# An S4 convolution and token mixer on one core: where the first half's transform back, its reads and the weights' splits stand

## The chip, the core and the metric

The kernel runs on one NeuronCore of a Trainium2 chip. The core has five engines that each work through their own list of instructions: TensorE (PE; its weight loads are shown as PEld), VectorE (DVE), ScalarE (ACT), GpSimd (POOL) and SyncE (SP). They wait for one another by semaphores. ScalarE, SP and POOL also issue DMAs, each on a queue of its own. The metric is the device time of one execution in microseconds.

## The reference

Everything is float32. B = 1, L = S = 2048, D = 512, N = 128, F = 1376.

```python
def _A_ref(u, A_re, A_im, B_re, B_im, C_re, C_im, log_dt, Dskip):   # S4 as a convolution
    dt = jnp.exp(log_dt)[:, None]
    A, Bc, Cc = A_re + 1j * A_im, B_re + 1j * B_im, C_re + 1j * C_im
    P = jnp.exp((dt * A)[:, :, None] * l[None, None, :])
    K = jnp.einsum("dn,dnl,dn->dl", Cc, P, dt * Bc).real
    # K and u are padded to 2L, their spectra multiplied, the product transformed back, cut to L
    return y + u * Dskip
def _B_ref(x, w1, w2, w3, w4):
    h = _gelu(_layernorm(x) @ w1)
    # four quarters of the channels are shifted by +1, -1, +2, -2 in time
    x1 = x + shifted @ w2
    return x1 + _gelu(_layernorm(x1) @ w3) @ w4
mod = (_silu(c) @ w_mod).reshape(c.shape[0], 6, 1, -1)             # sa, ca, ga, sb, cb, gb
x = A_u
x = x + ga * _A_ref(_layernorm(x) * (1 + ca) + sa, ...)
return x + gb * _B_ref(_layernorm(x) * (1 + cb) + sb, w1, w2, w3, w4)
```

## The kernel before, in words

The order of nearly all instructions is written out by hand (`tc.manual_schedule()`): an engine executes what its list says in the order of the program text, and only waits are put in by the framework.

**Stage 1** (to about 209 us) builds the convolution's kernel K in KX and the first transform of u, which goes to DRAM (VU). A table `side` (L506 and below) puts other work into its 32 rounds; among it are copies of w2, w3 and w4 from their input tensors to DRAM scratch (WD), issued by POOL.

**Stage 2** (209 to about 313 us) is the convolution in the frequency domain. `k_first` (L619), called eight times, transforms K into VK0 and VK1, with evictions by ScalarE and VectorE. Then sixteen steps follow, (jh, kc) for the two halves of the channels jh and eight blocks kc of frequencies. In step n the text has:

- `spectrum_k` (L664): TensorE's second transform of K, into psb banks. It uses T2 and its negative T3, which POOL writes (`flip`, L658).
- `multiply` (L685): six VectorE instructions, four products (ma, mb) and two sums (zc).
- `back` (L695) of step n-1: TensorE's transform of zc with Gm into psa banks (pz), ScalarE's eviction into z, and POOL's two DMAs of z to DRAM (ZT). There are two z buffers, so an eviction waits until the store of two steps earlier has landed.
- `spectrum_u` (L642) of step n+1: TensorE's transform of a VU block, which SP had loaded (`load_vu`, L638) into one of seven buffers ld, and ScalarE's three evictions (us).

The x that the result is added to (four DMAs, `load_x`, L723), FI, w1, w2 and the reads of ZT (`load_inv`, L717) are also issued by SP between the steps. `inverse` (L739) is the last transform back: `inv_half` (L726) multiplies blocks of ZT with FI on TensorE, and VectorE adds the result to x in X2 (which lies in KX). For the first half jh = 0 there are four parts g, each reading four of the eight ZT blocks: parts 0 and 3 read k = 0, 3, 4, 7 and parts 1 and 2 read k = 1, 2, 5, 6. Parts 0 and 3 stand in steps 12 and 13, part 1 in step 15, part 2 behind the steps.

Weights are split for TensorE into a high half (ScalarE writes it, w1h) and a low half (VectorE subtracts, w1l): `weights`, L743, with `load` and `split`. w1 is loaded in steps 8 and 9 into ld blocks and split in steps 9 and 10. w2 is loaded in step 12 and split in steps 14 and 15.

**The hole.** Behind step 15 its z must be stored and read back before anything of the second half jh = 1 can be transformed. In the meantime there are the transform back of (0, 2), statistics, and `keep` (L1162), matmuls whose results nobody reads.

**Stage 3** mixes tokens in eight groups of two blocks (`mix_mod1`, `mix_mod2`, `mix_norm`, `transposed`, `parts_of`, `mix_half`): the modulation and statistics on VectorE, the norm (h), the gelu (go) and the high half of the transposed norm (nh) on ScalarE, and the product with w1 on TensorE. go goes through DRAM (GD) and comes back shifted (win, `chan_load`); `chan_split` splits it (wh on ScalarE, the low half on VectorE), `chan_sum` multiplies it with w2. **Stage 4** (from about 375 us) is the channel MLP with w3 and w4.

Of the kernel before, what the change touches and what calls it, by code (L numbers as in the profile page):

```python
# [106 lines left out]
def body(ctx, tc, A):  # L107
# [12 lines left out]
    WD = {k: dpool.tile(list(A[k].shape), F32, name="D" + k) for k in ("w2", "w3", "w4")}  # L120
# [390 lines left out]
    for k in range(2):  # L511
        side[28 + 3 * k].append(lambda i=k * 256: P.dma_start(WD["w2"][i:i + 256], A["w2"][i:i + 256]))
# [94 lines left out]
    Gm = c2.tile([128, 2, 64], F32, name="Gm")  # L607
# [3 lines left out]
    ldp = a2.enter_context(pool("ldp", bufs=7))  # L611
# [44 lines left out]
    t3s = {}  # L656

    def flip(kc):  # L658
        t = t3s[kc] = c2.tile([128, 8, 64], F32, name="T3", bufs=3)
        for gh in range(2):  # L660
            r = slice(gh * 64, gh * 64 + 64)
            P.tensor_scalar(t[r], T2[kc // 4][r, kc % 4 * 4:kc % 4 * 4 + 8, 64 - gh * 64:128 - gh * 64], -1.0, None, op0=OP.mult)

    def spectrum_k(jh, kc):  # L664
        p = [kbank([128, 2, 2, 128]) for gh in range(2)]
        for i in range(2):
            for ro in range(2):
                for ri in range(2):
                    for kk in range(2):
                        for gh in range(2):  # L670
# [5 lines left out]
                            elif ro == ri:  # L676
                                w = w[:, gh * 64:gh * 64 + 64]
                            else:
                                w = t3s[kc // 2 * 2][rows, k1 % 8]
# [15 lines left out]
    def back(jh, kc):  # L695
        zc = zcs.pop((jh, kc))
        z = s2.tile([128, 4, 256], F32, name="z")
# [19 lines left out]
    def load_inv(jh, k, i=None, q=Y):  # L717
        if (jh, k) not in zis:
            zis[jh, k] = block()
# [3 lines left out]
    def load_x(g):  # L723
        Y.dma_start(X2[:, g * 4:g * 4 + 4].rearrange("p b d -> p (b d)"), A["x"][g])
# [18 lines left out]
    def weights(pl, src, rows, cols, name, ntile):  # L743
# [3 lines left out]
        def load(stage, i, m=1, c0=0, c1=cols):  # L747
            n = min(128, rows - i * 128)
            w = stage(m, c1 - c0) if stage else lo.bitcast(F32)[:, i:i + m, c0:c1]
            Y.dma_start(w[:n], src[i * 128:i * 128 + (m - 1) * 128 + n, c0:c1].rearrange("(a p) n -> p a n", p=n))  # L750

            def split():
                for j in range(m):
                    h = hi[:n, i + j, c0:c1]
                    act(h, w[:n, j])
                    V.tensor_sub(lo[:n, i + j, c0:c1], w[:n, j], h.bitcast(F32))  # L756
            return split
        return hi, lo, load

    def two(m, n):  # L760
        return block().rearrange("p (a c) b -> p a (c b)", a=2)
# [330 lines left out]
    def split_w(n):  # L1092
        for _ in range(n):
            splits.pop(0)()

    steps = [(jh, kc) for jh in range(2) for kc in range(8)]
    with tc.manual_schedule():
        load_vu(*steps[0])
        flip(0)
        Y.dma_start(Gm, A["G"].rearrange("p (a b) -> p a b", a=2))  # L1100
        for r in range(8):
            k_first(r)
            if r == 3:
                load_vu(*steps[1])
            if r == 6:
                load_vu(*steps[2])
        us = spectrum_u(*steps[0])
        split = None
        for n, st in enumerate(steps):
            p = spectrum_k(*st)  # L1110
            multiply(*st, us, p)
            if n == 7:
                v0x.close()
                pw2 = ctx.enter_context(pool("pw2", side="right", reuse_waits="tile"))
                pw1 = ctx.enter_context(pool("pw1", side="right", reuse_waits="tile"))
                W2h, W2l, ldw2 = weights(pw2, WD["w2"], 512, 512, "w2", 4)
# [185 lines left out]
```

## Time and profile before

| | us |
|---|---|
| median of 3 runs (lowest, highest) | 690.18 (689.29, 690.67) |
| profiled execution | 691.26 |
| its span | 689.5 |
| TensorE busy | 642.6 (93%) |
| VectorE busy | 498.0 (72%) |
| ScalarE busy | 331.2 (48%) |
| POOL busy | 124.8 (18%) |
| DMA: bytes moved, mean rate over the span | 86.42 MB, 125 GB/s |
| granted TensorE clock, mean of the span | 0.989 |

The engines' busy times overlap, and a busy TensorE is not TensorE at its peak, since matmuls are pipelined and their ends are modelled. The shares are means over four stages with different limits; what an edit is worth is read from its own stage. Times in the rows are microseconds from the start of the span. The last brackets of a row give the idle time of the engine ahead of the instruction and what ended it.

### The profile page before, as it was taken

To read this page: it belongs to the slowest core of one execution; us is meant where nothing else is said; L and a number is where in the kernel's file an instruction comes from. 1 tells how busy PE (TensorE), PEld (TensorE's weight loads), DVE (VectorE), ACT (ScalarE), POOL (GpSimd) and SP (SyncE) were. 2 spreads that over 40 slices of the span, in tenths; PEclk is the share of its full clock that TensorE was granted. 3 is DMA by queue.
4 is the path that set the end of the run, shared out by engine and by line. 5 is a ranking of instruction groups with operands and counts; after the bars stand their busy time and mean duration, and the time that the engine had idled before them with its cause. 6 is when DMAs were issued, how large, how long until landed. Compare 5 with 4: busy or idle time off the path is not lost.

```text
span 689.5 us, 16884 instructions
## 1 busy us (share of the span) xinstructions
PE 642.6 (93%) x7195; PEld 509.2 (74%) x7195; DVE 498.0 (72%) x795; ACT 331.2 (48%) x505; POOL 124.8 (18%) x236
## 2 busy tenths in 40 slices
PE   1899999999999998977998999999999999999996
PEld 0456655655569776634887889999899889898895
DVE  7899999999996887986987967464574536363522
ACT  3878988889875557432444623123131312222121
POOL 4011112112103355413741101001010000000000
PEclk9999999999999999998999999999999999999999
DMA  8603264643739997967387010020100201010001
GB/s 299 284 2 79 75 218 105 209 121 85 275 85 317 354 335 258 346 204 226 108 257 240 1 32 32 16 77 15 47 31 17 77 1 62 1 49 13 1 31 31
DMA packets 51091, 86.42 MB, mean 125 GB/s; under 512 B 4676, under 2 KB 39496, under 8 KB 48424
## 3 DMA queue, kind: packets, MB, share of 16 engines
q1 hardware_dynamic: 46712, 66.74, 30.1%
q0 software_dynamic: 3440, 17.57, 7.4%
q8 instruction: 56, 0.92, 0.6%
q10 hardware_dynamic: 864, 1.05, 0.5%
q14 instruction: 19, 0.16, 0.1%
HBM read 59.12 MB, written 32.90 MB: 133 GB/s over the span
## 4 chain that ended last, share of the span: by engine, by line
PE 70%; DVE 6%; DMA 5%; ACT 3%; POOL 2%; issue 1%; ACTq 0%; SPq 0%; DVEq 0%; POOLq 0%
PE pm L841 7%; PE pm L838 7%; PE pm L839 7%; PE xx L448 7%; PE pa L954 6%; PE pa L955 6%; PE pa L962 6%; PE kp L498 3%; DMA ZT<-z 3%; PE ph L893 2%; PE ph L895 2%; PE ph L892 2%; DMA ld<-ZT 2%; PE pu L426 2%; PE pT L803 2%; PE pk L626 2%
## 5 line engine op out<-in xcount | busy, mean ns | idle before, releaser
L115 ACT ACTIVATE gh<-pm 128x512 fp32r<-128x512 f32 (+1 forms) x48 | 26.9, 560 | 200.7 <-PE pm L841 200.7
L838 PE MATMUL pm<-nh,w3h 128*128 128x256 f32 (+1 forms) x352 | 86.6, 281 | 2.7 <-ACT nh L115 2.7
L839 PE MATMUL pm<-nh,w3l 128*128 128x256 f32 (+1 forms) x352 | 86.3, 280 | 0.1
L946 DVE TENSOR_TENSOR gl<-gf,gh 128x512 fp32r<-128x512 f32 (+1 forms) x48 | 30.8, 643 | 68.4 <-ACT gf L115 68.4
L954 PE MATMUL pa<-w4h,gh 128*128 128x512 f32 (+1 forms) x176 | 69.6, 395 | 0.0
L838 PEld LDWEIGHTS pm<-nh,w3h 128*128 128x128 f32 (+1 forms) x352 | 66.0, 187 | 4.4 <-ACT nh L115 2.9
L955 PE MATMUL pa<-w4l,gh 128*128 128x512 f32 (+1 forms) x176 | 68.9, 392 | 0.0
L839 PEld LDWEIGHTS pm<-nh,w3l 128*128 128x128 f32 (+1 forms) x352 | 65.9, 187 | 2.2 <-DVE w3l L756 0.5
L765 POOL TENSOR_TENSOR rs<-mv,eps_t 128x1 f32<-128x1 f32 (+1 forms) x39 | 11.0, 282 | 282.4 <-DVE mv L771 265.4
L841 PE MATMUL pm<-nl,w3h 128*128 128x256 f32 (+1 forms) x352 | 55.0, 278 | 0.0
L449 PE MATMUL xx<-MG,ON 64*128 64x512 f32 x160 | 48.1, 397 | 0.0
L962 PE MATMUL pa<-w4h,gl 128*128 128x512 f32 (+1 forms) x176 | 48.0, 390 | 0.0
L448 PE MATMUL xx<-MG,ON 64*128 64x512 f32 x160 | 48.0, 396 | 0.0
L841 PEld LDWEIGHTS pm<-nl,w3h 128*128 128x128 f32 (+1 forms) x352 | 47.0, 187 | 0.0
L898 DVE TENSOR_TENSOR h<-h,ph 128x512 f32<-128x512 f32 x16 | 11.0, 687 | 45.1 <-PE ph L895 45.1
L466 DVE SCALAR_TENSOR_TENSOR e<-tr,p 128x512 f32<-128x512 f32 x64 | 41.1, 684 | 1.5 <-ACT tr L115 1.5
L498 PEld LDWEIGHTS kp<-e,e 128*32 128x32 f32 x2048 | 30.1, 110 | 12.7 <-issue 7.6
L475 DVE TENSOR_TENSOR e<-tr,p 128x1024 f32<-128x1024 f32 x32 | 39.0, 1220 | 0.0
L476 DVE TENSOR_TENSOR e<-tr,m 128x1024 f32<-128x1024 f32 x32 | 39.0, 1219 | 0.0
L115 ACT ACTIVATE p<-xx 128x1024 f32<-128x1024 f32 (+1 forms) x40 | 37.5, 979 | 2.2 <-PE xx L252 1.0
L962 PEld LDWEIGHTS pa<-w4h,gl 128*128 128x128 f32 (+1 forms) x176 | 33.0, 188 | 7.3 <-DVE gl L946 0.2
L115 ACT ACTIVATE tr<-xx 128x1024 f32<-128x1024 f32 x32 | 33.0, 1030 | 9.6 <-PE xx L449 7.9
(236 smaller groups left out, 1731.6 us busy)
## 6 DMA issues: line engine op xcount, KB each, us to landing
VU<-vs SPq DMA_DIRECT2D x64, 128.0 KB, 3.7
ld<-VU SPq DMA_DIRECT2D x16, 512.0 KB, 7.4
ZT<-z POOLq DMA_DIRECT2D x30, 256.0 KB, 6.2
ld<-ZT SPq DMA_DIRECT2D x12, 512.0 KB
Dw<-in_w POOLq DMA_DIRECT2D x8, 688.0 KB, 4.7
xu<-in_u SPq DMA_DIRECT2D x4, 1024.0 KB, 8.0
KX<-in_x SPq DMA_DIRECT2D x4, 1024.0 KB, 8.0
GD<-go SPq DMA_DIRECT2D x16, 256.0 KB, 2.3
```

The costliest lines, as they stand in the source:

```text
L115: return S.activation(out, in_, f, bias=bias, scale=scale)
L448: T.matmul(x[:, :512], la, ma, start=(i == 0), stop=(i == len(ops) - 1))
L449: T.matmul(x[:, 512:], lb, mb, start=(i == 0), stop=(i == len(ops) - 1))
L466: V.scalar_tensor_tensor(e0[:, 1, a], tr[:, 1, 0], 1.0 - 2.0 * a, mg[:, a], op0=OP.mult, op1=OP.mult)
L475: V.tensor_mul(e0[:, 0], tr[:, 0, 0:1].to_broadcast([128, 2, 512]), mg)
L498: T.matmul(kp[32 * j:32 * j + 32, (k % 2) * 4 + g], e1[:, r, d], e0[:, r, :, d * 32:d * 32 + 32], start=(r == 0), stop=(r == 1), skip_grou ...
L838: T.matmul(p, wh[:, k, c], hi[k], start=(k == 0), stop=False)
L839: T.matmul(p, wl[:, k, c], hi[k], start=False, stop=False)
L841: T.matmul(p, wh[:, k, c], lo[k], start=False, stop=(k == 3))
L954: T.matmul(acc[i], gh[:m, e, s], W4h[:m, f], start=(f == 0), stop=False)
L955: T.matmul(acc[i], gh[:m, e, s], W4l[:m, f], start=False, stop=False)
L962: T.matmul(acc[i], gl[:m, e, s], W4h[:m, f], start=False, stop=(f == 10))
```

## The change

What moves, by place:

- **Stage 1**: w1 is copied to DRAM scratch as w2 is. The four copies of halves stand in rounds 24, 26, 28 and 30.
- **Start of stage 2**: both flips of all of T2 are done at once (eight POOL instructions of 64x512, into one T3 tile). Before there were sixteen, since the second half's steps negated T2 again: one pair ahead of the steps and one in each even step up to 12. VU blocks 1 to 3 are loaded during `k_first`, then FI. Gm now lies in the buffer of FK, so SP's load of it waits for `k_first`.
- **Steps**: VU is loaded four steps ahead instead of three, with six ld buffers instead of seven. x is loaded by POOL in steps 0, 2, 4 and 6. There are three z buffers. w1 is loaded by POOL, in steps 8 and 9, from the scratch copy straight into w1l. All reads of ZT of the first half stand in steps 11 and 12, behind the last VU blocks in SP's list; k = 0, 3, 4, 7 have buffers of their own (zi, in VK0's place).
- **Last steps**: part (0, 0) stands in step 14 and (0, 3) in step 15, (0, 1) behind `back` of step 15. Of w1's split only ScalarE's half stands in steps 13 and 14.
- **Hole**: part (0, 1), and VectorE's half of w1's split. SP issues all reads of the second half.
- **Mixing**: w2 is loaded behind these reads; ScalarE's four instructions stand behind the first half of group 1, VectorE's four behind the first half of group 2.

POOL's list from the first flips through the first steps, before. T3 is the negated table, xu are the two halves of T2, ZT0 is the first half's scratch, and z is named with its buffer:

```order
L662 TENSOR_SCALAR T3_3081<-xu_2528 64x512 x2
L662 TENSOR_SCALAR T3_3355<-xu_2528 64x512 x2
L706 DMA ZT0_61<-z_3402 32x2x1024 x2
L706 DMA ZT0_61<-z_3473 32x2x1024 x2
L662 TENSOR_SCALAR T3_3500<-xu_3042 64x512 x2
L706 DMA ZT0_61<-z_3547 32x2x1024 x2
L706 DMA ZT0_61<-z_3619 32x2x1024 x2
L662 TENSOR_SCALAR T3_3646<-xu_3042 64x512 x2
L706 DMA ZT0_61<-z_3694 32x2x1024 x2
L706 DMA ZT0_61<-z_3765 32x2x1024 x2
```

The same place of POOL's list now (KX is where x goes):

```order
L662 TENSOR_SCALAR T3_3079<-xu_2530 64x512 x4
L662 TENSOR_SCALAR T3_3079<-xu_3045 64x512 x4
L724 DMA KX_88<-in_x 128x2048
L706 DMA ZT0_61<-z_3412 32x2x1024 x2
L706 DMA ZT0_61<-z_3483 32x2x1024 x2
L724 DMA KX_88<-in_x 128x2048
L706 DMA ZT0_61<-z_3555 32x2x1024 x2
L706 DMA ZT0_61<-z_3626 32x2x1024 x2
L724 DMA KX_88<-in_x 128x2048
L706 DMA ZT0_61<-z_3698 32x2x1024 x2
```

The flips stand ahead of the first store, and an x load stands ahead of every second step's store.

TensorE's list at the end of the steps, before. The first pair is `back` of step 14, zc_4494 and zc_4495 are step 15's, pk is part (0, 1), py is part (0, 2):

```order
L702 MATMUL pz<-zc_4421,Gm 64x512 x2
L702 MATMUL pz<-zc_4422,Gm 64x512 x2
L731 MATMUL pk_4515<-ld,FI 32x256 x8
L731 MATMUL pk_4524<-ld,FI 32x256 x8
L702 MATMUL pz<-zc_4494,Gm 64x512 x2
L702 MATMUL pz<-zc_4495,Gm 64x512 x2
L731 MATMUL py<-ld,FI 32x256 x16
```

The same place now (Gm lies in FK's buffer and has its name; zc_4448 and zc_4449 are step 15's):

```order
L702 MATMUL pz<-zc_4353,FK 64x512 x2
L702 MATMUL pz<-zc_4354,FK 64x512 x2
L731 MATMUL pz<-zi,FI 32x256 x16
L702 MATMUL pz<-zc_4448,FK 64x512 x2
L702 MATMUL pz<-zc_4449,FK 64x512 x2
L731 MATMUL pk_4502<-ld,FI 32x256 x8
L731 MATMUL pk_4511<-ld,FI 32x256 x8
L731 MATMUL py<-ld,FI 32x256 x16
```

Part (0, 3), in the pz banks that `back` uses too, has come between the two `back`, and part (0, 1) has gone behind the last.

ScalarE's list in the mixing, before, from the gelu (go) of the first half of group 1 to the split of win:

```order
L115 ACTIVATE go<-pm 128x512
L115 ACTIVATE h_4980<-h_4980,nm,rs 128x512 x2
L115 ACTIVATE go<-pm 128x512
L115 ACTIVATE nh_5153<-pT_5143 128x512
L115 ACTIVATE nh_5154<-pT_5144 128x512
L115 ACTIVATE go<-pm 128x512
```

The same place now (h_4961 is the norm of group 2, as h_4980 was):

```order
L115 ACTIVATE go<-pm 128x512
L115 ACTIVATE w2h<-w2l 128x512 x4
L115 ACTIVATE h_4961<-h_4961,nm,rs 128x512 x2
L115 ACTIVATE go<-pm 128x512
L115 ACTIVATE nh_5138<-pT_5128 128x512
L115 ACTIVATE nh_5139<-pT_5129 128x512
L115 ACTIVATE go<-pm 128x512
```

Four w2h have come ahead of group 2's norm.

The diff, cut to its core:

```diff
     for k in range(2):
-        side[28 + 3 * k].append(lambda i=k * 256: P.dma_start(WD["w2"][i:i + 256], A["w2"][i:i + 256]))
+        for j, w in enumerate(("w1", "w2")):
+            side[24 + 4 * j + 2 * k].append(lambda w=w, i=k * 256: P.dma_start(WD[w][i:i + 256], A[w][i:i + 256]))
...
-    ldp = a2.enter_context(pool("ldp", bufs=7))
+    ldp = a2.enter_context(pool("ldp", bufs=6))
...
-        z = s2.tile([128, 4, 256], F32, name="z")
+        z = s2.tile([128, 4, 256], F32, name="z", bufs=3)
...
-            zis[jh, k] = block()
+            zis[jh, k] = block() if jh or k in (1, 2, 5, 6) else zip_.tile([128, 4, 256], F32, name="zi")
...
     def load_x(g):
-        Y.dma_start(X2[:, g * 4:g * 4 + 4].rearrange("p b d -> p (b d)"), A["x"][g])
+        P.dma_start(X2[:, g * 4:g * 4 + 4].rearrange("p b d -> p (b d)"), A["x"][g])
...
         flip(0)
-        Y.dma_start(Gm, A["G"].rearrange("p (a b) -> p a b", a=2))
+        flip(1)
         for r in range(8):
             k_first(r)
-            if r == 3:
-                load_vu(*steps[1])
+            if r in (1, 3, 5):
+                load_vu(*steps[r // 2 + 1])
             if r == 6:
-                load_vu(*steps[2])
+                Y.dma_start(FI, A["FI"].rearrange("p (a b c) -> p a b c", a=32, b=2))
+        Gm = pa12.tile([128, 2, 64], F32, name="FK")
+        Y.dma_start(Gm, A["G"].rearrange("p (a b) -> p a b", a=2))
...
             if n > 0:
                 back(*steps[n - 1])
-            if n == 15:
-                i1 = inverse_parts(0, 1, psb, "pk2")
             if n < 15:
                 us = spectrum_u(*steps[n + 1])
-            if n + 3 < 16:
-                load_vu(*steps[n + 3])
-            if n % 2 == 0 and n < 14:
-                flip(steps[n + 2][1])
-            if n in (3, 4, 6, 8):
-                load_x(n - 3 if n < 5 else n // 2 - 1)
-            if n == 9:
-                Y.dma_start(FI, A["FI"].rearrange("p (a b c) -> p a b c", a=32, b=2))
-            if split:
-                split()
-                split = None
+            if n + 4 < 16:
+                load_vu(*steps[n + 4])
+            if n in (0, 2, 4, 6):
+                load_x((0, 3, 1, 2)[n // 2])
             if n in (8, 9):
-                split = ldw1(two, n % 2 * 2, 2)
-            if n == 10:
+                w1s.append(ldw1(None, n % 2 * 2, 2, q=P))
+            if n in (13, 14):
+                w1s[n - 13] = w1s[n - 13]()
+            if n == 11:
                 for k in (0, 3, 4, 7):
                     load_inv(0, k)
             if n == 12:
+                for k in (1, 2, 5, 6):
+                    load_inv(0, k)
+            if n == 14:
                 inverse(0, 0)
-                w2s = [ldw2(None, 2 * i, 2) for i in range(2)]
                 for b in range(4):
                     half_stat(b, 0)
-            if n == 13:
+            if n == 15:
                 inverse(0, 3)
-                for k in (1, 2, 5, 6):
-                    load_inv(0, k)
-            if n in (14, 15):
-                w2s.pop()()
-        for f in i1:
-            f()
         back(*steps[15])
+        i1 = inverse_parts(0, 1, psb, "pk2")
...
         for k, i in ((3, 1), (0, 0)):
             load_inv(1, k, i, Y)
-            load_inv(1, k + 4, i, S)
+            load_inv(1, k + 4, i, Y)
...
+        for f in i1:
+            f()
         for i in range(2):
             inv_half(0, 2, i, psy, "py")()
         for b in (14, 15, 4, 5, 6, 7):
             half_stat(b, 0)
+        for f in w1s:
+            f()
         for k in (1, 2):
             load_inv(1, k)
             load_inv(1, k + 4)
+        w2s = ldw2(None, 0, 4)
...
         mix_half(1, hl, 0)
+        w2s = w2s()
         mix_norm(2)
...
         mix_half(2, hl, 0)
+        w2s()
         chan_split(0)
```

44 lines of the change are left out of this document (23 added, 21 removed).

## The prediction

> **What bounds the kernel now.** I began with the page's chain, which lies on TensorE for 70% of the span. That is an average over stages with different limits, so I then read the chain piece by piece between 205 and 330 us, where everything lies that the change touches. Its columns are start, length, engine and line.
>
> ```profile
> 234.17 8.87 DMA ZT<-z
> ...
> 252.91 8.02 DMA ZT<-z
> ...
> 303.75 0.60 ACT z L115
> 304.37 0.62 ACTq L706
> 305.03 2.69 DMA ZT<-z
> 307.94 0.41 ACTq L721
> 308.51 4.98 DMA ld<-ZT
> ...
> 313.63 2.42 PE py L731 x17
> ```
>
> Two things are to be seen. Inside the sixteen steps the chain goes twice through a store of z of over 8 us, though the same store takes 2.69 us when nothing else is in flight. And after the last step there is a hole: the last z is evicted by 304.35, stored, read back, and TensorE goes on at 313.63.
>
> Next, what the steps cost on VectorE, from the groups of its instructions between 227 and 302.1 us (count, busy us, mean ns, idle time ahead of them) and from its timeline.
>
> ```profile
> L690 DVE TENSOR_TENSOR ma<-pk,us 128x512 f32<-128x512 f32 x32 | 21.9, 684 | 8.9 <-ACT us L115 5.9 <-PE pk L680 2.6 <-issue 0.5
> ...
> L756 DVE TENSOR_TENSOR w1l<-ld,w1h 128x512 fp32r<-128x512 f32 x4 | 3.0, 788 | 1.0 <-ACT w1h L115 1.0
> L734 DVE TENSOR_TENSOR KX<-pz,KX 128x512 f32<-128x512 f32 x4 | 2.6, 685 | 0.0
> L756 DVE TENSOR_TENSOR w2l<-w2l,w2h 128x512 fp32r<-128x512 f32 x3 | 2.0, 689 | 0.3 <-ACT w2h L115 0.3
> L784 DVE BATCH_NORM_STATS2 st<-KX 128x6 f32<-128x256 f32 x4 | 1.4, 416 | 0.0
> ```
> ```profile
> 227.31 0.69 DVE L690 TENSOR_TENSOR ma<-pk,us 128x512 f32<-128x512 f32 x1 [2.12 <-PE pk L680]
> ...
> 230.91 0.69 DVE L690 TENSOR_TENSOR ma<-pk,us 128x512 f32<-128x512 f32 x1
> ...
> 234.82 0.69 DVE L690 TENSOR_TENSOR ma<-pk,us 128x512 f32<-128x512 f32 x1 [0.23 <-PE pk L680]
> ...
> 248.29 1.10 DVE L692 TENSOR_TENSOR zc<-mb 128x512 f32<-128x512 f32 x1
> ...
> 252.31 0.68 DVE L692 TENSOR_TENSOR zc<-mb 128x512 f32<-128x512 f32 x1
> ...
> 301.36 0.69 DVE L692 TENSOR_TENSOR zc<-mb 128x512 f32<-128x512 f32 x1
> ```
>
> A step is six VectorE instructions. Two steps start 3.60 us apart (227.31, 230.91), or 3.91 (to 234.82) when TensorE is late. From 227.31 to the end of the last zc at 302.05 the sixteen steps take 74.7 us; at 3.60 they would take 57.6. The other 17 us are the rows above: 8.9 of idle time ahead of the products, the weights' low halves (w1l with its wait 4.0, w2l 2.3), the first half's adds and statistics (2.6 and 1.4), and zc instructions that ran slower beside POOL's flips (1.10 against 0.69). Who causes the idle time stands in ScalarE's waits and timeline.
>
> ```profile
> ACT z L115 <- DMA ZT<-z: 8.7, 3, 4.3
> ```
> ```profile
> 254.20 1.08 ACT L115 ACTIVATE z<-pz 128x512 f32<-128x512 f32 x2 [0.69 <-PE pz L702]
> 255.17 1.59 ACT L115 ACTIVATE us<-pk 128x512 f32<-128x512 f32 x3
> ```
>
> ScalarE's eviction of z waits until the store of two steps earlier has landed, and the us of the next step stands behind it. So these steps are bound by VectorE where transfers let them, and by the transfers where not.
>
> **The steps in the new order.** I build the stage up again. The products need 16 x 3.6 = 57.6 us. But from the end of one step's zc (252.99) over TensorE's transform, the z and the us to the end of that us (256.76), which the next products but one need, lie 3.77 us. So I take 3.8 per step, between the 3.60 and 3.91 of the rows: 60.8. Of the other work only the adds and statistics of inverse(0, 0) still stand between two products (half of 2.6, and 1.4): 2.7. The last zc then ends at 227.31 + 60.8 + 2.7 = 290.8 instead of 302.05: **11.2 us less**, bounds 8 (every step 3.91, and 0.1 for each of the two w1h pairs) and 14.4 (every step 3.60). The start stays:
>
> ```profile
> L662 POOL TENSOR_SCALAR T<-xu 64x512 f32<-64x512 f32 x16 | 24.6, 1536 | 27.3 <-DMA wm<-in_TU 26.2
> ```
>
> k_first is the same, and the eight flips of 1.54 us run beside its copies as four did before. Gm's load now waits for k_first to have read FK, and behind it on SP's queue stand the fifth VU block and all later ones; four steps of 3.8 us lie between that point and the step that reads the fifth, so I cost it at 0. If they came later than that, each us would count.
>
> A new wait comes in. Part 3's transform (0, 3) now uses the psa banks just ahead of back(15), and VectorE adds them only behind the last zc. The two adds are 0.6 apart, the last two matmuls of back(15) need the second: **1.0 us more**, bounds 0.6 and 1.2. Behind it queue the last z, its store and the hole.
>
> **The transfers.** Here is the term that I know least.
>
> ```profile
> 242.00:247.00 5.00, 4.16 (x77) 2.35 (x70) 1.81 (x4) 3.55 (x8) 1.14 (x2) 1.00 1.06 409
> ...
> 277.00:282.00 5.00, 3.98 (x92) 3.27 (x87) 5.00 (x9) 2.56 (x5) 2.11 (x3) 1.00 1.05 350
> ```
> ```profile
> 222.00:302.00 80.00, 72.85 (x1542) 54.36 (x1541) 69.20 (x115) 46.39 (x90) 35.15 (x42) 1.00 0.93 317
> ```
> ```profile
> ld<-VU SPq DMA_DIRECT2D x16, 512.0 KB, 7.4
> ZT<-z POOLq DMA_DIRECT2D x30, 256.0 KB, 6.2
> ...
> KX<-in_x SPq DMA_DIRECT2D x4, 1024.0 KB, 8.0
> ```
>
> The last two columns of a window are the busy share of the DMA engines and GB/s. Full windows carry 350 to 409, say 370; the stage as a whole carries 317, which is 25.4 MB in 80 us. In the new order 23.6 MB are left at 222: twelve VU blocks (6.3), the stores of z (7.9), x (4.2), w1 (1.0) and ZT of the first half (4.2). FI has gone ahead into k_first, w2 behind the hole. At 370 that ends at 286, at 317 at 296.5: as tight as the engines' 290.8. A z buffer now has three steps less its eviction and its issue, 11.4 - 2.2 = 9.2 us, to land. Every second store has an x load of 1.05 MB ahead of it on POOL's queue, 1.57 MB together, while SP's queue takes 0.52 MB per 3.8 us = 138 GB/s. That leaves POOL 370 - 138 = 232 or 317 - 138 = 179 GB/s: 6.8 or 8.8 us and the 2.7 of an empty store, so 0.3 or 2.3 us too late, for three x loads (the first has nothing behind it): 0.9 to 6.9. I take **3.5 us more**, near the middle, since no row has x on POOL's queue.
>
> That x and w1 now go out by POOL adds six issues to it:
>
> ```profile
> L706 POOL DMA_DIRECT2D ZT<-z x30: 528/550/632, 233.5 to 300.1; - x30
> ```
>
> Its 30 stores were issued in 0.53 to 0.63 us each (least, median, most) beside a VectorE that was busy 69.2 of 80 us, so I cost an issue at 0.55 us of a POOL that then has nothing else to do: 0. The Trainium skill ("SBUF — State Buffer", SBUF: two separate sides) speaks against the move: VectorE can lock GpSimd out while it writes the descriptors of its DMAs. By that rule six issues would wait for up to a VectorE instruction each, as an estimate some 4 us; the even issue times do not bear it out.
>
> **The hole.**
>
> ```profile
> 306.33 2.05 DVE L784 BATCH_NORM_STATS2 st<-KX 128x6 f32<-128x256 f32 x6
> 316.07 0.69 DVE L734 TENSOR_TENSOR KX<-py,KX 128x512 f32<-128x512 f32 x1 [7.69 <-PE py L731]
> ```
>
> VectorE is idle for 7.69 us there. The four w1 low halves (4 x 0.6 = 2.4) fit in, and so does the transform (0, 1) on TensorE, as long as the one of the 325.52 row below (1.9), since TensorE too does nothing but a few keep-warm products between the transform (0, 2) and 313.63: 0. If that cover were gone, they would cost 2.4. The four reads that TensorE waits for are now all issued by SP, about 0.4 us each, where ScalarE issued two: **0.3 more**, bounds 0 and 0.8. With six ld blocks instead of seven, two of the last reads (k = 2 and 6) wait for the transform (1, 3), where one did:
>
> ```profile
> 312.63 7.85 SPq L721 DMA_DIRECT2D ld<-ZT  x4
> ```
> ```profile
> 325.52 1.93 PE L731 MATMUL py<-ld,FI 128*32 128x256 f32 x32
> ```
>
> The last was out by 320.5; one more of 0.5 MB lands 1.5 us later at 350 GB/s, close to when TensorE wants it at 325.5: **0.3 more**, bounds 0 and 1.5.
>
> **w2 in the mixing.**
>
> ```profile
> 348.05 0.60 ACT L115 ACTIVATE go<-pm 128x512 f32<-128x512 f32 x1 [5.00 <-PE pm L841]
> 348.54 1.72 ACT L115 ACTIVATE h<-h,nm,rs 128x512 f32<-128x512 f32 x2
> 350.81 0.60 ACT L115 ACTIVATE go<-pm 128x512 f32<-128x512 f32 x1 [0.55 <-PE pm L841]
> ...
> 357.91 1.22 DVE L879 TENSOR_TENSOR win<-win,wh 128x1024 fp32r<-128x1024 f32 x1 [2.46 <-ACT wh L115]
> ```
> ```profile
> 296.46 1.18 ACT L115 ACTIVATE w2h<-w2l 128x512 fp32r<-128x512 f32 x2
> ```
>
> Four w2h (2.3 us) now stand between the go of 348.05 and the h behind it; that h feeds the transposes of group 2, and TensorE has no spare time around it. ScalarE's 0.55 us of idle time takes part of it: **1.6 more**, bounds 0 and 2.4. The four w2l fall into VectorE's idle 2.46: 0.
>
> **The sum.** -11.2 + 1.0 + 3.5 + 0.3 + 0.3 + 1.6 = -4.5. The profiled execution took 691.26 (span 689.5 and 1.8 around it), so it would take 686.8; the median of the runs shown is 690.18, 1.1 lower: **685.7 us**.
>
> **The rivals.**
>
> (1) The transfers set the pace, at the 317 GB/s they have now: the last zc ends at 296.5, not at 290.8 + 3.5. For it speaks that the bytes are nearly the same. Against it:
>
> ```profile
> 267.00:272.00 5.00, 4.46 (x97) 3.73 (x97) 3.99 (x7) 3.58 (x7) 3.84 (x4) 1.00 0.33 94
> ```
>
> The mean holds a stretch at 94 GB/s in which VU blocks stood on SP's queue behind reads that waited for stores, and in the new order no VU block stands behind them. Time: 685.7 + 2.2 = 687.9.
>
> (2) The engines set it: no late store, 3.60 per step. For it speak 227 to 242 us, where three of four steps were 3.60; against it the busy DMA. Time: 685.7 - 3.5 - 3.2 = 679.0.
>
> (3) Slower: POOL's queue starves. A store behind an x load waits for x first, and x shares with SP's queue. The 8.87 us store moved 0.5 MB, 59 GB/s of some 330, while SP's queue was full. If x takes the 8.0 us of its row and the store its 6.2 behind it, each of the three comes 14.2 - 9.2 = 5.0 late, 15 in all in place of 3.5: 697.2. It makes the kernel slower from 3.1 us late at each (9.4 in all), which is POOL's queue at under 1.57 / (9.2 + 3.1 - 2.7) = 164 GB/s; against it, SP's queue now carries one block per step and not x, FI and w1. The Trainium skill ("DMA: Bandwidth & Descriptors", Queues, rings and completion order) says that engines alternate between queues packet by packet and that one queue's work starts in order, which is this mechanism; by that rule, and the trace's 59 GB/s agrees, what is put ahead of a store on its own queue costs most.
>
> (4) The change doesn't do what it says: the third buffer helps nothing, since TensorE and ScalarE take turns at 4.3 us per step. For it speaks that TensorE was busy 72.85 of 80 us, against it the first steps. Then 16 x 0.5 = 8 of the 11.2 us stay, but the stores have time (3.5 less): 690.2.
>
> **How the numbers follow.** The forecast (682.5 to 687) has 0.49, rival (1) 0.20, (2) 0.17, (3) 0.07, (4) 0.07. From the bounds, 679 (rival 2) to 690.2 (rival 4, or late stores of 6.9 and w2 at 2.4 together) holds 8 in 10. About 0.2% is what a measurement of this kernel can tell from no change, 688.8 to 691.6. Faster: 0.47 + 0.18 + 0.17 + 0.02 = 0.84. Same: 0.02 + 0.02 + 0.04 = 0.08. Slower: 0.08.
>
> **What would show it.** In the new profile ScalarE's z waits for ZT<-z are few and short, steps start 3.6 to 3.9 apart, no weight stands between them, and the last zc ends near 294. The hole still takes about 10 us from the last z to the first py. ScalarE has w2h ahead of h in the mixing. The forecast is wrong if z waits for stores above 5 us in total (rival 3 from 15), if the steps stay above 4.2 us without such waits (4), or if the stage behind the hole grows by more than 3 us.

## The result

| | kernel before | kernel after |
|---|---|---|
| median, us (six runs each) | 689.39 (687.31 to 690.67) | 685.07 (683.56 to 685.86) |
| profiled execution, us | 691.26 | 685.86 |
| its span, us | 689.5 | 684.0 |
| first product to the end of the last zc, us | 74.7 | 67.0 |

The ratio is 0.9938 with a 95% interval of 0.9919 to 0.9957: 0.6% faster, where 685.7 us was forecast. The sum was right; one of its terms stands for something that did not happen, and something not foreseen is as large.

### The profile page after: what moved, and what is told of

It is laid out like the page before. It is cut to its first block, busy times and chain, and to the rows that moved or that the text cites. A ratio compares the mean times of both kernels' runs of the same rounds, so it can differ in the third digit from the quotient of the medians.

```text
span 684.0 us, 16869 instructions
## 1 busy us (share of the span) xinstructions
PE 634.6 (93%) x7195; PEld 507.9 (74%) x7195; DVE 496.9 (73%) x795; ACT 331.0 (48%) x505; POOL 117.1 (17%) x236
## 4 chain that ended last, share of the span: by engine, by line
PE 74%; DMA 4%; DVE 4%; ACT 2%; issue 2%; POOL 1%; SPq 0%; DVEq 0%; ACTq 0%; POOLq 0%
PE pm L838 7%; PE pm L839 7%; PE xx L448 7%; PE pm L841 7%; PE pa L954 6%; PE pa L955 6%; PE pa L962 6%; PE kp L498 4%; PE pk L680 4%; PE pu L426 2%; PE pz L702 2%; PE ph L893 2%; PE ph L892 2%; PE ph L895 2%; PE pk L650 2%
## 5 line engine op out<-in xcount | busy, mean ns | idle before, releaser
L448 PE MATMUL xx<-MG,ON 64*128 64x512 f32 x160 | 47.1, 390 | 0.0
L449 PE MATMUL xx<-MG,ON 64*128 64x512 f32 x160 | 47.1, 390 | 0.0
```

The costliest lines, as they stand in the source:

```text
L448: T.matmul(x[:, :512], la, ma, start=(i == 0), stop=(i == len(ops) - 1))
L449: T.matmul(x[:, 512:], lb, mb, start=(i == 0), stop=(i == len(ops) - 1))
```

## The profile after

ScalarE's waits inside the steps come first (226 to 298 us; total, times, longest), with the group of VectorE's products (226.5 to 294).

```profile
ACT z L115 <- PE pz L702: 22.9, 15, 2.4
ACT z L115 <- issue: 4.2, 1, 4.2
```
```profile
L690 DVE TENSOR_TENSOR ma<-pk,us 128x512 f32<-128x512 f32 x32 | 21.9, 683 | 8.3 <-PE pk L680 8.3
```

No eviction of z waits for a store any more, where 8.7 us did before. All of VectorE's idle time ahead of the products, 8.3 us, now ends with spectrum_k: TensorE is late. Of these, 2.1 us lie ahead of the first product, as in the kernel before (2.12), so 6.2 us fall inside the steps. VectorE's timeline shows where, and TensorE's shows how.

```profile
253.46 0.68 DVE L690 TENSOR_TENSOR ma<-pk,us 128x512 f32<-128x512 f32 x1
...
258.34 0.69 DVE L690 TENSOR_TENSOR ma<-pk,us 128x512 f32<-128x512 f32 x1 [1.20 <-PE pk L680]
...
263.19 0.69 DVE L690 TENSOR_TENSOR ma<-pk,us 128x512 f32<-128x512 f32 x1 [1.17 <-PE pk L680]
...
266.79 0.69 DVE L690 TENSOR_TENSOR ma<-pk,us 128x512 f32<-128x512 f32 x1
...
271.46 0.69 DVE L690 TENSOR_TENSOR ma<-pk,us 128x512 f32<-128x512 f32 x1 [0.99 <-PE pk L680]
...
293.20 0.68 DVE L692 TENSOR_TENSOR zc<-mb 128x512 f32<-128x512 f32 x1
293.80 1.28 DVE L734 TENSOR_TENSOR KX<-pz,KX 128x512 f32<-128x512 f32 x2
```
```profile
248.68 0.33 PE L680 MATMUL pk<-VK,xu 64*64 64x128 f32 x3 [0.21 <-issue]
...
255.40 1.09 PE L650 MATMUL pk<-ld,wm 64*64 64x256 f32 x16 [0.72 <-issue]
...
261.76 0.27 PE L680 MATMUL pk<-VK,T 64*64 64x128 f32 x1 [1.15 <-issue]
...
267.54 0.38 PE L680 MATMUL pk<-VK,xu 64*64 64x128 f32 x2 [0.99 <-issue]
...
279.69 0.27 PE L680 MATMUL pk<-VK,T 64*64 64x128 f32 x1 [1.24 <-issue]
```

The first six steps take 3.83 us on average, as forecast; the next eight take 4.27. The last zc ends at 293.88. In the slower stretch TensorE stops five times (0.21, 0.72, 1.15, 0.99, 1.24: 4.3 us), four times in the middle of a spectrum_k, between products that wait for nothing new. The view puts that down to "issue": nothing that it shows released them. But TensorE's instructions can be counted. A DMA queue that the trace calls the instruction queue brings them, in transfers of 16,384 bytes, and if an instruction takes 64 bytes, 256 of them fill one. Here is each block of 256 TensorE instructions (weight loads, products and semaphore waits), laid so that one begins at 261.76, beside those transfers (times in us, from the trace's records):

```
block begins   transfer of the next: starts    ends     next block begins
232.15         233.03                          234.14   236.94
236.94         237.52                          240.63   242.80
242.80         246.38                          247.32   248.68   stop of 0.21
248.68         252.94                          254.03   255.40   stop of 0.72
255.40         259.29                          260.39   261.76   stop of 1.15
261.76         265.06                          266.13   267.54   stop of 0.99
267.54         270.74                          271.67   273.27
273.27         277.17                          278.08   279.69   stop of 1.24
279.69         283.76                          284.83   286.24
286.24         288.96                          290.02   292.76
292.76         293.24                          294.21   311.11
```

Every stop ends exactly where a new block begins, 1.36 to 1.61 us after that block's transfer ended. From 242.80 to 286.24 all seven blocks begin within 1.36 to 1.61 us of that end: TensorE takes each as it arrives. The transfer starts 3.2 to 4.3 us after the block ahead of it has begun, where 0.5 to 0.9 is to be seen for the blocks begun at 232, 237 and 293 (from 227 to 242 us the engines moved 291 GB/s). So a block takes 5.7 to 6.7 us, and a step, which has 176 instructions, at least 3.9 to 4.6. In the kernel before, the same count for the blocks begun between 246 and 279 gives starts of 0.05 to 4.0 us, and at least 2.75 us from a transfer's end to the next block: no stop.

The DMA engines are fuller there (windows of before, then after; the last column is GB/s):

```profile
247.00:287.00 40.00, 36.24 (x779) 27.69 (x774) 36.07 (x60) 24.15 (x47) 23.89 (x27) 1.00 0.89 299
```
```profile
247.00:287.00 40.00, 35.68 (x817) 28.63 (x813) 34.27 (x57) 25.61 (x51) 12.08 (x22) 1.00 1.04 372
```

SP's blocks of VU take longer to land too, 12.8 us from their issue where it was 6.8 in the same stretch (222 to 302 us, before, then after: count, size, median to landing). They are now asked for a step earlier, and no wait of TensorE in the steps ends at such a landing.

```profile
ld<-VU SPq DMA_DIRECT2D x9, 512.0 KB, 6.8
```
```profile
ld<-VU SPq DMA_DIRECT2D x12, 512.0 KB, 12.8
```

Behind the steps: the hole (ScalarE's timeline, then the chain) and the mixing (ScalarE's timeline of after, and one row of before).

```profile
296.31 1.09 ACT L115 ACTIVATE z<-pz 128x512 f32<-128x512 f32 x2 [4.24 <-issue]
```
```profile
302.47 4.65 DMA ld<-ZT
...
307.26 1.97 PE py L731 x16
```
```profile
341.80 0.60 ACT L115 ACTIVATE go<-pm 128x512 f32<-128x512 f32 x1 [4.99 <-PE pm L841]
342.30 2.18 ACT L115 ACTIVATE w2h<-w2l 128x512 fp32r<-128x512 f32 x4
344.38 1.51 ACT L115 ACTIVATE h<-h,nm,rs 128x512 f32<-128x512 f32 x2
345.79 0.58 ACT L115 ACTIVATE go<-pm 128x512 f32<-128x512 f32 x1
...
366.99 0.60 ACT L115 ACTIVATE go<-pm 128x512 f32<-128x512 f32 x1 [8.43 <-DMA GD<-go]
```
```profile
371.71 0.60 ACT L115 ACTIVATE go<-pm 128x512 f32<-128x512 f32 x1 [7.66 <-PE pT L803]
```

The first py comes 6.37 us earlier than before (313.63), the go at 341.80 comes 6.25 earlier (348.05), the next 5.02 (350.81), and that of 366.99 comes 4.72 earlier (371.71). So the mixing gives 1.5 back, 1.2 of it at the place where four w2h stand ahead of h.

## The experiments

The theory (A) is that TensorE's next 256 instructions come too late while the data queues are full, and that this sets the pace from 242 us on. The rivals are that the engines' own loop sets it (B), or that the data of the steps come late (C).

**Less data.** The four lines that load x are taken out.

```diff
-            if n in (0, 2, 4, 6):
-                load_x((0, 3, 1, 2)[n // 2])
```

> The four loads of x are left out (4.2 MB; X2 then holds what K left, so the values are not the reference's). In the changed kernel's trace five gaps of TensorE inside the steps (0.21, 0.72, 1.15, 0.99 and 1.24 us) end at 248.68, 255.40, 261.76, 267.54 and 279.69; from one to the next lie 256 instructions of TensorE (twice 256 before the last), and each ends 1.37 to 1.6 us after the end of a transfer of 16,384 bytes on the queue that brings instructions. Theory A (instructions): TensorE's next block of 256 instructions waits 3.2 to 4.3 us in the queue behind the data, so a block takes 5.7 to 6.7 us and a step (176 instructions) 4.0 to 4.6. Without x the delay falls to the 0.5 to 2 us seen outside of the full stretch, the gaps go, steps start 3.6 to 3.9 apart up to step 14, the last zc ends near 290 instead of 293.9, and the kernel takes about 681.5 us, 0.988 to 0.990 of the kernel before. Theory B (the engines' own loop of transform, z and us sets 4.2 us per step): nothing moves, 0.9938. Theory C (VU blocks land late): the same gain as A, but the gaps that remain do not end at the landing of instructions.

Measured: 681.2 us, 0.9872 (0.9844 to 0.99). TensorE's waits between 226 and 262 us are one row, and it is busy for 35.52 of these 36 us, while the DMA engines move 277 GB/s:

```profile
PE pz L702 <- DVE zc L692: 0.5, 1, 0.5
```
```profile
226.00:262.00 36.00, 35.52 (x847) 30.32 (x843) 35.07 (x59) 23.89 (x47) 9.88 (x18) 1.00 0.89 277
```

The blocks begun between 241 and 257 start their transfers 0.8 to 2.4 us in and stop nothing; steps take 3.60 and 3.91 in turn up to 262. Behind 263, where w1 and the first half's reads load the queues, the delays are 3.4 to 4.2 again, and two stops (0.53 and 1.51) end 1.42 and 1.35 us behind a transfer. The steps gain 2.4 us of 67.0. That the first product also came 1.65 us earlier has no reason in this edit (it came between 225.2 and 228.4 in the profiled runs). B falls, since the same loop ran faster; C does not yet.

**Fewer instructions, the same data.**

```diff
         for i in range(2):
-            for ro in range(2):
...
+            for ri in range(2):
+                for kk in range(2):
+                    for gh in range(2):
+                        k1 = kc * 4 + 2 * kk + i
+                        rows = slice(gh * 64, gh * 64 + 64)
+                        T.matmul(p[gh][:, i, kk], T2[k1 // 16][rows, k1 % 16],
+                                 VK[jh][rows, ri * 32 + k1].rearrange("p j g -> p (j g)"),
+                                 start=(ri == 0), stop=(ri == 1), skip_group_check=True)
```

> Half as many products in spectrum_k with the same work for TensorE: one product with 128 columns of weights (both values of ro) in place of two with 64, which run two side by side instead of four; T3 is not read. The values are not the reference's. TensorE then has 112 instructions per step instead of 176; all transfers stay. Theory A (instructions): a block of 256 lasts 2.3 steps, 8.6 us at 3.75 per step, above the 6.7 that its transfer can take: no gap ends behind an instruction transfer, steps start 3.6 to 3.9 apart, the last zc ends near 290, total about 681.5 (0.988 to 0.990). If transfers then bind, ScalarE's z waits for stores again (over 1 us in total). Theory B (engines): unchanged, 0.9938. Theory C (data): unchanged steps of 4.2 us, TensorE still idle ahead of spectrum_u or spectrum_k, 0.993 to 0.995.

Measured: 681.54 us, 0.9885 (0.9862 to 0.9909), no stop behind an instruction transfer, no z that waits for a store. A block lasts 8.5 to 9.2 us, and its successor has arrived 4.0 us or more before it ends. The timeline of VectorE and the window of the steps:

```profile
253.11 0.69 DVE L682 TENSOR_TENSOR ma<-pk,us 128x512 f32<-128x512 f32 x1 [0.19 <-PE pk L672]
...
256.99 0.69 DVE L682 TENSOR_TENSOR ma<-pk,us 128x512 f32<-128x512 f32 x1 [0.20 <-PE pk L672]
...
260.86 0.69 DVE L682 TENSOR_TENSOR ma<-pk,us 128x512 f32<-128x512 f32 x1 [0.19 <-PE pk L672]
```
```profile
226.00:290.00 64.00, 62.62 (x904) 42.83 (x900) 61.23 (x103) 40.49 (x79) 19.31 (x35) 1.00 0.97 346
```

Steps are 3.88 us, all transfers arrive at 346 GB/s instead of 332, and VU blocks land after 7.9 us where they took 12.8. The merged products do not shorten the engines' loop: with twice as many products, in the kernel without x, undisturbed steps took 3.60 and 3.91 in turn. So neither the data (C) nor the engines' loop (B) held the steps at 4.27: TensorE's instructions did. The two runs together settle it.

**The third buffer alone.**

```diff
-        z = s2.tile([128, 4, 256], F32, name="z", bufs=3)
+        z = s2.tile([128, 4, 256], F32, name="z")
```

> The changed kernel with two store buffers for z instead of three; all else stays. Theory A (instructions set the pace from 242 us on): a buffer then has two steps of 4.3 us less 2.2 for the eviction and the issue, 6.4 us, and a store takes 6.4 in the median and longer behind x: ScalarE waits for ZT<-z two to four times, 3 to 6 us in total, part of which the late instructions would have cost anyway: 1 to 4 us slower than the changed kernel, 0.995 to 1.000 of the kernel before. Rival: the store waits hide all of the instruction waits (the pace is the transfers' anyway): within 0.5 us of the changed kernel, 0.993 to 0.9945.

Measured: 688.69 us, 1.0 (0.9985 to 1.0015).

```profile
ACT z L115 <- DMA ZT<-z: 17.0, 6, 4.3
```

Six evictions wait for stores, 17.0 us in total. The steps take 70.7 us instead of 67.0, and all of the change's gain is gone. The stops behind instructions (3.4 us) hide little of it. The time is at the far end of the expected range, and the rival falls.

**Where x is queued, how much is queued, how large the DMAs are.** Three edits ask why an instruction block starts late.

```diff
-        P.dma_start(X2[:, g * 4:g * 4 + 4].rearrange("p b d -> p (b d)"), A["x"][g])
+        Y.dma_start(X2[:, g * 4:g * 4 + 4].rearrange("p b d -> p (b d)"), A["x"][g])
```

> The loads of x go back to SP's queue, ahead of the VU blocks of the same step; the stores stand alone on POOL's. Theory A1 (instructions wait longest where both data queues are backlogged): POOL's queue is empty between two stores, the delay of an instruction block falls from 3.2-4.3 us towards the 2.2 that the kernel before had, the gaps that end behind an instruction transfer fall from 4.3 us to under 2, total 1.5 to 3 us less (0.990 to 0.992). Theory A2 (the fullness of the DMA engines decides, whatever the queue): the gaps stay at 3 to 5 us, total within 1 us of the changed kernel, or slower where VU blocks stand behind x.

```diff
-            if r in (1, 3, 5):
+            if r in (1, 3):
...
-            if n + 4 < 16:
-                load_vu(*steps[n + 4])
+            if n + 3 < 16:
+                load_vu(*steps[n + 3])
```

> VU blocks are asked for three steps ahead instead of four, so SP's queue holds a block less. Theory A1 (the delay of an instruction block comes from how much stands in the data queues ahead of it): the gaps behind instruction transfers fall by a quarter or more, under 3.3 us in all. Theory A2 (it comes from the share that the queues get while both have work, however much stands in them): they stay at 3.8 to 5.3 us.

```diff
-        Y.dma_start(t, dram(VU, jh * 1048576 + kc * 8 * 16384, [[256, 128], [32768, 4], [1, 256]]))
+        for a in (0, 2):
+            Y.dma_start(t[:, a:a + 2], dram(VU, jh * 1048576 + kc * 8 * 16384 + a * 32768, [[256, 128], [32768, 2], [1, 256]]))
...
-                    load_inv(0, k)
+                    load_inv(0, k, 0)
+                    load_inv(0, k, 1)
```

> On top of the two edits of the run before the last: each VU block and each read of the first half's ZT is asked for by two DMAs of 256 KB instead of one of 512; bytes, queues and the size of the single packets (1 KB) stay. Open is why an instruction block starts 3 to 4 us late while the data queues are full. Theory P (an instruction block waits for a whole DMA's run of packets on its engine, 32 of 46 ns = 1.5 us for a VU block): the delay falls by 0.7 us or more, the gaps from the 6.2 us of the two edits to under 3, total 680 to 681 us (0.986 to 0.988 of the kernel before). Theory Q (it comes from how full the engines are, not from the size of the DMAs): gaps of 4 to 6.5 us as before, 682 to 684 us (0.990 to 0.992).

The three beside the others, for the steps of each profiled run (stops: those that end 1.15 to 1.75 us behind an instruction transfer; delay: mean from a block's begin to the start of its successor's transfer, blocks begun between 241 and 282 us):

```
                        stops, us   delay, us   first product to last zc   GB/s
before                  0           1.90        74.7                       313
after                   4.3         3.74        67.0                       332
without x               2.0         2.81        64.6                       294
fewer instructions      0           2.66        64.0                       346
two buffers for z       3.4         3.96        70.7                       315
x on SP's queue         4.5         2.96        67.2                       345
VU three steps ahead    5.7         3.65        68.3                       334
after, once more        5.7         3.96        68.1                       327
two edits (below)       6.2         4.00        68.7                       324
the same, halved DMAs   4.4         3.72        67.2                       329
```

With x on SP's queue (684.99 us, 0.9937, 0.9918 to 0.9957) the stops come earlier, four of the five between 238 and 260, and their sum stays. Its mean delay is low only because the late blocks now begin earlier: from 227 to 259 us, at 375 GB/s, the delay is 3.2 to 4.3.

VU asked for later (one run, 685.36) does not lessen the stops; their 5.7 us lie above the range of A2 too, but the changed kernel itself had 5.7 in its other profiled run. There the VU blocks land after 8.8 us instead of 12.8, so much of their longer way is the earlier asking. DMAs of half the size leave the delay within the spread of 3.6 to 4.0 (682.32 us, 0.9885, 0.9863 to 0.9907).

So the first two of these runs speak for A2 and the third for Q: neither the queue, nor how much stands in it, nor the size of the DMAs moved the sum of the stops. Leaving out x moved it, and so did fewer instructions. How full the engines are is not all of it either: with fewer instructions they moved 375 GB/s between 241 and 282 us, where the changed kernel has 369, and the delay was 2.2 to 3.8 us.

**The wait in front of the last z.**

```diff
             if n == 15:
-                inverse(0, 3)
+                i3 = inverse_parts(0, 3, psa, "pk1")
         back(*steps[15])
+        for f in i3:
+            f()
```

> The transform (0, 3) goes to the two pk1 banks (free after the last spectrum_u) and its two adds stand behind back(15), so back(15) no longer waits for them. Theory A and the prediction's term: back(15) starts 0.97 us earlier, right behind the last zc, all behind it too: 0.9 to 1.2 us less than the changed kernel, 0.992 to 0.993 of the kernel before if the others are as measured (ratio of the changed kernel 0.9938). Rival: the wait is hidden in the hole by the issue and landing of the reads, which wait for the transforms (0, 1) and (0, 2) and not for the last z: under 0.3 us less.

Measured: 684.82 us, 0.9929 (0.9906 to 0.9952), not to be told from the changed kernel by time. In the trace the last z ends 2.29 us behind the last zc instead of 3.51, as in the kernel before (2.29): 1.2 us. The first py follows that z after 10.51 us instead of 9.87, so 0.6 is left, and 0.2 against the changed kernel's other profiled run (9.53). This kernel's chain shows where the rest goes: it runs over TensorE's `keep` products up to a read that is issued at 301.17, and the reads take 5.26 us instead of 4.65.

```profile
299.57 1.60 PE pT L1162 x6
301.17 0.32 SPq L721
...
302.10 5.26 DMA ld<-ZT
```

**w2h earlier in the mixing.**

```diff
+        w2s = w2s()
         mix_half(1, hl, 0)
-        w2s = w2s()
         mix_norm(2)
```

> The four w2h copies stand ahead of the go of group 1's first half, in the 4.99 us that ScalarE waits there for TensorE, instead of behind it and ahead of h of group 2. Theory (the prediction's w2 term of 1.6 us, of which the traces show 1.25 at the next go and up to 1.9 by 400 us): the time between the go of group 1's first half and its second half falls from 3.99 to 2.8 us and 1.2 to 1.9 us are gained: 0.991 to 0.992 of the kernel before. Rival: the loss between 341 and 400 us comes from elsewhere (the clock, the stores of go), and moving w2h gains under 0.4 us: 0.9935 or more.

```profile
344.74 0.60 ACT L115 ACTIVATE go<-pm 128x512 f32<-128x512 f32 x1 [2.92 <-PE pm L841]
345.23 1.72 ACT L115 ACTIVATE h<-h,nm,rs 128x512 f32<-128x512 f32 x2
347.51 0.60 ACT L115 ACTIVATE go<-pm 128x512 f32<-128x512 f32 x1 [0.55 <-PE pm L841]
```

The two go are 2.77 us apart instead of 3.99, as in the kernel before (2.76). From the first go of the mixing (327.49 here, 324.28 in the changed kernel) to the one that stands there at 366.99 pass 40.6 us instead of 42.7. In the changed kernel's other profiled run it is 42.2, and in the two kernels below that also have w2h earlier it is 40.2 and 40.7. The median did not show the gain: 686.16 us, 0.9936 (0.991 to 0.9961), which is the rival's range; in the profiled run, steps and start had come 2.4 us later. So by time it is open, and by the traces it is 1.6 to 2.1 us.

**w1 in the hole**, alone and with the two edits above.

```diff
-            if n in (8, 9):
-                w1s.append(ldw1(None, n % 2 * 2, 2, q=P))
-            if n in (13, 14):
-                w1s[n - 13] = w1s[n - 13]()
+            if n == 15:
+                w1s = [ldw1(None, 2 * i, 2, q=P) for i in range(2)]
...
         for f in w1s:
-            f()
+            f()()
```

> The two loads of w1 (1.05 MB) are issued in step 15 instead of steps 8 and 9, and the four w1h copies stand behind the last z, in the hole, ahead of the w1l there. Theory A: between 262 and 280 the DMA engines carry 1 MB less, which takes one or two of the instruction gaps (0.7 to 1.3 us each) away, and step 15 no longer waits for a w1h pair (0.7 us); w1h and w1l (2.3 and 2.4 us) fit in ScalarE's and VectorE's idle time of some 10 and 7 us: 1 to 2 us less than the changed kernel, 0.991 to 0.9925. Rival: w1 lands among the last stores and reads of the hole and makes its 9.9 us longer by what the steps gain: 0.9935 to 0.995.

> Three edits together: the adds of the transform (0, 3) behind back(15), w2h ahead of the go of group 1, and w1 in the hole. Theory A with the terms as the traces show them: 0.6 + 1.3 to 2.6 + 1 to 2 = 3 to 5 us less than the changed kernel: 680 to 682 us, 0.987 to 0.989 of the kernel before. Rival: the gains meet in the hole (w1, the reads and the adds) and only that of w2 is left: 0.991 to 0.992.

Measured: 684.09 us, 0.9928 (0.9913 to 0.9943), and 684.26 us, 0.9935 (0.9918 to 0.9952). With w1 alone the stops stay at 4.7 us, although 1 MB has left the steps, and the time lies between the two expected ranges. With all three edits the stops are 3.4 us, and the time lies above even the rival's range. The chain of that kernel shows the rival's cause, that the gains meet in the hole: the last store takes 5.43 us (2.69 in the kernel before) beside w1, and the first py comes 12.7 us behind the last z instead of 9.9.

```profile
295.60 5.43 DMA ZT<-z
```

**Two edits, beside the changed kernel.** The adds behind back(15) and w2h earlier, w1 left in its place; and the changed kernel once more on the same chip.

> The changed kernel itself once more, beside the next one on the same chip: 0.992 to 0.996 of the kernel before. Theory A: its TensorE has again gaps of 3.5 to 5.5 us in all that end 1.3 to 1.7 us behind an instruction transfer, between 242 and 282 us; by chance (the rival) they would not come again, or end elsewhere.

> The adds of the transform (0, 3) behind back(15), and w2h ahead of the go of group 1; w1 as in the changed kernel. From the traces of the two edits alone: 0.6 us at the first py and 1.25 at the next go but one, up to 2.6 by 430 us: 1.9 to 3.2 us less than the changed kernel on the same chip, 0.989 to 0.991 of the kernel before. Rival (the median of the run with w2h alone): the mixing gives nothing lasting, 0.6 us less at most.

The changed kernel: 685.63 us, 0.995 (0.9929 to 0.997), with stops of 5.7 us, all between 252 and 280. The two edits: 683.05 us, 0.9905 (0.9871 to 0.9939), 2.6 us less than the changed kernel beside it, as expected, though its stops (6.2 us) happened to be the longest of all. With the halved DMAs on top it is the 682.32 us above, the fastest kernel here that leaves nothing out: 2.8 and 3.3 us under the changed kernel's two medians (not taken on one chip), with an interval below both of its intervals. That halving itself helps is not shown.

## Why the prediction came out

**The steps.** The 3.8 us per step (60.8) and 2.7 for inverse(0, 0) were right as long as nothing else came: 64.0 with fewer instructions and 64.6 without x, against 63.5. Of the 11.2 us less, the trace had 8.2, 0.4 of them from an earlier start. Two readings on the way were off and did not enter the sum. Of the 8.9 us of idle time that were to explain the steps of before, 2.1 lie ahead of the first product. And the lower bound of 8 should be 9.2 by its own working (16 steps of 3.91, 2.7 and 0.2).

**The late stores: the step that failed.** "I take 3.5 us more, near the middle, since no row has x on POOL's queue": no z waited for a store at all, and the three buffers held even behind x. A store was to need 9.5 to 11.5 us behind x, with 9.2 at hand; it needed at most 8.3 (least, median and most of all stores, from issue to landing):

```profile
DMA to landing us min/median/max: 2.6/6.3/8.3
```

In its place stands what the prediction had nowhere: 4.3 us of stops for instructions. That both are near 4 is chance, and so the time was right in part by luck. The prediction's own sign of being wrong, steps above 4.2 us without waits for stores, came true in eight of the steps (4.27). The step failed because it asked which data would be late when the queues fill, and not what else is brought by DMA: TensorE's instructions.

**Where the third buffer's worth lies.** With it the steps take 67.0 us, without it 70.7, and the kernel then runs as long as before (1.0). The change's other moves gain the other 4.1 us of the steps (74.7 to 70.7), and what stands behind the steps takes most of that back: with two buffers the last zc ends 4.6 us earlier than before (297.42), but the go that stands at 366.99 in the changed kernel comes only 1.3 us earlier (370.37).

**The new wait**: 1.0 forecast (0.6 to 1.2), 1.2 in the trace, as its removal shows. **The hole**: 0.3 and 0.3 forecast; from the end of the last z to the first py 9.87 us instead of 9.29, so 0.6 where the first 0.3 was to be (9.53, so 0.2, in the other profiled run). The second 0.3 did not come, the late reads of k = 2 and 6 cost nothing that is to be seen: the go of 324.28 is 6.27 us earlier than its counterpart, like the first py. w1l in the hole was free: it ran from 302.68 to 305.16, ahead of the first py. **w2 in the mixing**: 1.6 forecast, 1.5 measured by the go of 366.99 (1.1 in the other profiled run), and the edit that moves w2h takes it back. **The issues on POOL**: 0 forecast; of the six, the first of x and the first of w1:

```profile
220.69 0.61 POOL L724 DMA_DIRECT2D KX<-in_x  x1
...
261.75 0.73 POOL L750 DMA_DIRECT2D w1l<-Dw  x1
```

They take 0.58 to 0.75 us each, and the stores 0.55 in the median as before. The Trainium skill's rule of VectorE locking GpSimd out while it writes descriptors ("SBUF — State Buffer", SBUF: two separate sides) shows in none of these issue times.

**The sum** was -4.5 against the profiled run, and -5.4 came, with -4.3 between the medians. The profiled run of before was 1.9 us above the median of its six runs. Of the 5.4 us, 0.7 arise behind the go of 366.99 (371.71 before), in code that is the same in both; why is open.

**The rivals.** (1) The transfers at 317 GB/s set the pace: they ran at 332, and at 346 once instructions were fewer. (2) No late store was right, 3.60 per step was not. (3) POOL's queue did not starve; it was SP's blocks whose way to landing grew (12.8 us). (4) Steps above 4.2 without store waits did come, as that rival would show itself, but not by its cause (TensorE and ScalarE taking turns): with fewer instructions the turns take 3.88.

## What to carry to other kernels

A stage of many small products can be paced by the arrival of TensorE's instructions, as this one was. Count them per step, and where the DMA engines are full, compare the time of 256 of them with the some 6 us that a block took here. When a wait is removed and transfers move closer together, ask what else is brought by DMA, and not only whether the data arrive. The sign is a stop of TensorE in the middle of a run of equal products with no releaser, which ends a nearly fixed time behind a transfer on the instruction queue (1.2 to 1.65 us in these runs).

## What was not expected of the hardware

Between 242 and 286 us the instruction queue moved seven blocks, 0.1 of 16 MB, and these bound TensorE. The Trainium skill ("Runtime: NRT & Kernel Launch", Instruction fetch mechanics) says that a sequencer fetches blocks of 16 KiB, 256 instructions, by a DMA queue of its own, and that this is mostly hidden. The trace agrees on the block to the instruction. But it was not hidden here: there were 3.4 to 6.2 us of stops in each profiled run of the changed kernel, or of one close to it that kept x and the number of instructions. The page also gives TensorE room for 2,048 instructions; in the rows above the next block's transfer started only after the block ahead of it had begun.

Why the transfer starts late is not shown. The Trainium skill ("DMA: Bandwidth & Descriptors", Queues, rings and completion order) lets an engine drain a packet of descriptors from one queue before it turns to the next; asking for the VU blocks and the first half's reads by twice as many DMAs left the delay at 3.72 us (4.00 without), so if that is the cause, the size of a DMA is not its measure. Smaller rows within a store were not tried. Without x, while the engines moved 277 GB/s, the delay was 0.65 to 2.4 us; at 369 GB/s in the changed kernel it was 3.2 to 4.3; but with fewer instructions it was 2.2 to 3.8 at 375. So full engines go with the late start, and something besides them has a part in it.
